# One block's k shift on 32x32 tiles of TensorE, with its result turned back by DMA

## The chip, the cores and the metric

The kernel runs on one core of a Trainium2 chip. The metric is the device time of one execution, in microseconds (us); lower is better. A core has five engines, each with its own in-order instruction queue: TensorE (PE, matmuls from SBUF into PSUM), VectorE (DVE), ScalarE (ACT), GpSimd (POOL) and SyncE (SP, which in this kernel only issues DMAs). An instruction that waits holds everything behind it on its engine.

## The reference, cut to what matters

Two layer pairs are applied to `x = A_q` of 2048 rows and 512 columns. The first of a pair is a gated long convolution, the second a SwiGLU FFN. All arrays are bf16.

```python
x = x + A(layernorm(x), k, v, shift_k, ssm_k, ssm_D)
x = x + B(layernorm(x), w_gate, w_up, w_down)
x = x + A(layernorm(x), ...)        # the same k, v and weights again
x = x + B(layernorm(x), ...)

def A(q, k, v, shift_k, ssm_k, ssm_D):
    # per channel: a causal filter of 4 taps over the rows of k
    k_shift[s] = sum(k[s - j] * shift_k[:, j] for j in range(4))
    kv = k_shift * v
    y = causal_conv(kv, ssm_k)      # by FFT, 2048 taps per channel
    return q * (y + kv * ssm_D)

def B(x, w_gate, w_up, w_down):     # 512 -> 1792 -> 512
    return (silu(x @ w_gate) * (x @ w_up)) @ w_down
```

The convolution doesn't depend on x, so the kernel computes it once and uses it in both layers.

## The kernel before, in words

**Tiles.** The 2048 rows are cut into 4 blocks of 512 (`NB = 4`). Inside a block, row 4p + r lies on partition p in slot r (`R = 4`), so a tile of a block is 128 x 4 x 512. 512 channels are 4 groups `dt` of 128.

**The convolution** (`conv(c)`, for blocks c = 1, 2, 3; block 0 is written out ahead of it). For each block: `spectrum_h` turns and transforms the long filter `hn` into `H`, `spectrum_x` shifts k, multiplies it into v (`vt`, in place) and transforms the product into `X`: for each slot r two matmuls of 512 columns (`by_residue`, L638) and an evacuation from PSUM to SBUF (L525). Products of spectra (`product`) run on VectorE, and `inverse` turns the sum back into `Yk`.

**The k shift** comes in two forms. Blocks 0 and 1 use `shift_mul` (L603 and on): k lies transposed in `kTb` (channels on partitions, 512 rows of time on the free axis, 16 more in front). For each slot r, 16 matmuls of 128 columns multiply a strided slice of `kTb` (the weights) with a diagonal matrix `dg` of one tap; the result has rows on the partitions, as `vt` has. For block 1, ScalarE copies it to `ks` (L620), and VectorE multiplies it into one slot of `vt` (L621). Four slots: four groups, four copies, four multiplies. Blocks 2 and 3 use `shift_mul_t` (L705 and on): ScalarE scales, VectorE adds, and DMAs turn the sum, 128 x 512 each, SBUF to SBUF.

**Units.** A unit (layer, block, half) is 256 rows through `prologue` (x += n * y, statistics, the normalised `z`, its transpose `zT`) and `ffn` (14 tiles of `w_gate` and `w_up`, then `w_down`). The first unit's prologue turns z on TensorE (L1022 to L1027); all others turn it by DMA (L994). The first unit needs the whole of block 0's convolution: products on VectorE, `inverse_half` (L881 and on, the matmuls L895 into two banks of ring `pd` and two of `pf`), `Yk` (L815), then x (L1004 to L1009), statistics (L914, L915), a power on GpSimd (L905), z (L964).

**PSUM** is cut into rings: `pf` 4 banks, `pc` 2, `pd` 2. In block 1, `shift_mul` takes `pc` banks one after the other.

**The order of the work** isn't found while the program runs. Each call of `plan.add` makes an operation with an engine, a modelled cost and, for DMAs, a modelled landing time `lat`. The list `ORDER` has one number for each operation, in the order of the `add` calls: its place. `Plan.order` sorts by place; `Plan.walk` models the run to choose buffers, and has rules of its own for when a transfer lands. Each engine then gets its operations in the order of their places, SP among them. The numbers were found by a search outside of the file. So a place decides what stands ahead of what on an engine.

**SP's queue.** All large loads and all turns by DMA, but for three small ones, are issued by SP in one queue: the first loads (L448, L458, L488, L492), `w_gate` (L503), the two turned tables `inv` (L1382, SBUF to SBUF), `kTb` of block 1 (L460, turned while it is loaded), `w_up` (L503), two parts of `w_down` (L500; 512 KB and 1280 KB), x of block 1 (L492), and, for block 2, `hn`, `kTb` and `vt`.

Of the kernel before, what the change touches and what calls it, by code (L numbers as in the profile page):

```python
# [9 lines left out]
P = 128  # L10
# [20 lines left out]
STRASSEN={(1,2,1):4,(0,3,0):4,(0,3,1):4,(1,3,0):4,(1,3,1):2}  # L31
I_RING = lambda k: "pf" if k == 3 else "pc"
# [88 lines left out]
R = 4  # L121
# [222 lines left out]
def kernel(  # L344
# [14 lines left out]
    nc = tc.nc  # L359
# [1169 lines left out]
```

## Time and profile before

| what | before |
|---|---|
| median of 3 runs | 339.6 us (339.44 to 339.8) |
| span of the profiled execution, first to last instruction | 337.7 us |
| what the median has above that span | 1.9 us |
| TensorE busy | 330.9 us, 98% |
| VectorE busy | 299.9 us, 89% |
| ScalarE busy | 262.8 us, 78% |
| granted TensorE clock | 1.000 |

The profiled execution has no time of its own beside its span, so the median of the runs is set beside the span. In the lines of the profile, `L416` is the line of kernel.py that issued an instruction (here the helper `mm`), PEld is TensorE's load of weights, `x16` a count, and `ps<-dg,kTb` says what was written from what. A timeline line begins with the start and the duration in us; in square brackets stands the idle time of the engine in front, and what ended it. `SPq` is SP issuing a DMA; its duration is the time that the issue took, while the landing time counts from issue to data landed. A line of the view of waits gives the sum, the count and the longest. A line of the view of windows gives the length of the stretch, then for each engine its busy time and count, the granted clock, the busy share of the DMA engines and GB/s.

### The profile page before, as it was taken

To read this page: it belongs to the slowest core of one execution; us is meant where nothing else is said; L and a number is where in the kernel's file an instruction comes from. 1 tells how busy PE (TensorE), PEld (TensorE's weight loads), DVE (VectorE), ACT (ScalarE), POOL (GpSimd) and SP (SyncE) were. 2 spreads that over 40 slices of the span, in tenths; PEclk is the share of its full clock that TensorE was granted. 3 is DMA by queue.
4 is the path that set the end of the run, shared out by engine and by line. 5 is a ranking of instruction groups with operands and counts; after the bars stand their busy time and mean duration, and the time that the engine had idled before them with its cause. 6 is when DMAs were issued, how large, how long until landed. Compare 5 with 4: busy or idle time off the path is not lost.

```text
span 337.7 us, 5898 instructions
## 1 busy us (share of the span) xinstructions
PE 330.9 (98%) x2141; PEld 204.6 (61%) x2172; DVE 299.9 (89%) x512; ACT 262.8 (78%) x534; POOL 35.4 (10%) x48
## 2 busy tenths in 40 slices
PE   9999999999999999999999999999999999999996
PEld 7655864645445564745454464744455687858884
DVE  8899999999888998999999999999999787877545
ACT  7889999999967466999899894999675556475462
POOL 4050001102100000122010100011100100100000
PEclk9999999999999999999999999999999999999999
DMA  7999604632346147421324434510514230204101
GB/s 255 350 229 376 130 13 66 151 82 41 71 93 94 36 91 188 95 49 32 62 53 106 97 60 110 138 35 16 96 28 82 56 72 17 48 18 93 49 3 62
DMA packets 77993, 31.59 MB, mean 94 GB/s; under 512 B 69766, under 2 KB 75787, under 8 KB 77963
## 3 DMA queue, kind: packets, MB, share of 16 engines
q1 hardware_dynamic: 77808, 31.13, 39.6%
q8 instruction: 17, 0.28, 0.4%
q14 instruction: 14, 0.11, 0.1%
q10 hardware_dynamic: 154, 0.07, 0.1%
HBM read 12.33 MB, written 2.10 MB: 43 GB/s over the span
## 4 chain that ended last, share of the span: by engine, by line
PE 91%; ACT 4%; DMA 2%; issue 1%; DVE 1%; SPq 1%
PE pf L416 56%; PE pd L1210 20%; PE ps L1085 7%; PE ps L416 6%; DMA kTb<-in_A_k_dram 1%; PE wm L1495 1%; DMA sg<-hr 1%; ACT H L525 1%; SPq L1132 1%; ACT ks L620 1%; ACT n L959 0%; ACT jk L929 0%; DVE t L748 0%; ACT ev L525 0%; ACT hr L1124 0%
## 5 line engine op out<-in xcount | busy, mean ns | idle before, releaser
L416 PEld LDWEIGHTS <-zT 128*128 128x128 bf16 x528 | 51.6, 98 | 58.5 <-DMA zT<-z 0.2
L416 PE MATMUL pf<-wg_sb,zT 128*128 128x512 bf16 x255 | 64.3, 379 | 0.5
L416 PE MATMUL pf<-wu_sb,zT 128*128 128x512 bf16 x260 | 64.3, 379 | 0.2
L1210 PE MATMUL pd<-wd_sb,sg 128*128 128x512 bf16 x189 | 48.1, 379 | 0.9 <-DMA sg<-hr 0.3
L1124 ACT CAST hr<-pf 128x512 bf16<-128x512 f32 x66 | 38.4, 593 | 12.4 <-PE pf L416 8.5
L1123 ACT ACTIVATE sg<-pf 128x512 bf16<-128x512 f32 x66 | 38.8, 608 | 11.3 <-PE pf L416 10.2
L416 PE MATMUL pf<-zT,wg_sb 128*128 128x256 bf16 x368 | 46.0, 273 | 0.1
L416 PE MATMUL pf<-zT,wu_sb 128*128 128x256 bf16 x368 | 45.9, 273 | 0.0
L758 DVE TENSOR_TENSOR t<-X,G 128x4096 bf16<-128x4096 bf16 x18 | 40.9, 2284 | 0.1
L416 PEld LDWEIGHTS <-wu_sb 128*128 128x128 bf16 x368 | 36.0, 98 | 8.1
L416 PEld LDWEIGHTS <-wg_sb 128*128 128x128 bf16 x368 | 35.9, 98 | 7.9 <-issue 0.4
L1183 ACT ACTIVATE sg<-pf 128x512 bf16<-128x512 f32 x46 | 27.3, 607 | 10.8 <-PE pf L416 10.8
L1187 ACT CAST ht<-pf 128x512 bf16<-128x512 f32 x46 | 26.8, 595 | 9.8 <-PE pf L416 8.0
L905 POOL TENSOR_TENSOR rstd<-mv,nhalf 128x2 f32<-128x2 f32 x20 | 17.0, 852 | 158.2 <-DVE mv L915 134.7
L1210 PEld LDWEIGHTS <-sg 128*128 128x128 bf16 x200 | 19.5, 98 | 21.7 <-DMA sg<-hr 0.8
L1210 PE MATMUL pd<-wd_sb,ht 128*128 128x512 bf16 (+1 forms) x124 | 29.7, 369 | 0.1
L914 DVE BATCH_NORM_STATS2 bst<-xc 128x6 f32<-128x512 bf16 x40 | 26.5, 683 | 0.5
L905 POOL TENSOR_TENSOR rstd<-ve,nhalf 128x2 f32<-128x2 f32 x12 | 14.6, 1218 | 111.7 <-ACT ve L942 111.7
L1190 DVE TENSOR_TENSOR ht<-ht,sg 128x512 bf16<-128x512 bf16 (+1 forms) x31 | 16.6, 544 | 8.8 <-ACT sg L1183 4.5
L1130 DVE TENSOR_TENSOR hr<-hr,sg 128x1024 bf16<-128x1024 bf16 x27 | 18.4, 682 | 4.2 <-ACT sg L1123 2.0
L1210 PEld LDWEIGHTS <-ht 128*128 128x128 bf16 x126 | 12.3, 98 | 13.1 <-DVE ht L1190 0.3
L525 ACT ACTIVATE X<-ps 128x512 bf16<-128x512 f32 x32 | 18.4, 604 | 1.6 <-PE ps L416 0.9
(143 smaller groups left out, 522.1 us busy)
## 6 DMA issues: line engine op xcount, KB each, us to landing
hn<-in_A_ssm_k_dram SPq DMA_DIRECT2D x4, 512.0 KB, 3.7
vt<-in_A_v_dram SPq DMA_DIRECT2D x4, 512.0 KB, 5.5
xc<-in_A_q_dram SPq DMA_DIRECT2D x4, 512.0 KB, 5.6
out_dram<-xc SPq DMA_DIRECT2D x15, 128.0 KB, 1.9
wg_sb<-in_B_w_gate_dram SPq DMA_DIRECT2D x1, 1792.0 KB
wu_sb<-in_B_w_up_dram SPq DMA_DIRECT2D x1, 1792.0 KB, 8.9
wd_sb<-in_B_w_down_dram SPq DMA_DIRECT2D x1, 1280.0 KB, 12.1
sg<-hr SPq DMA_TRANSPOSE x66, 2.4
```

The source lines that it names most:

```text
L416: nc.tensor.matmul(o, lhsT=lhsT, rhs=rhs, start=(n == 0), stop=(n == len(terms) - 1))
L525: add("ACT", act(D), lambda: nc.scalar.activation(out=view(), in_=ps.t[:], func=ACT.Copy, scale=scale), r=[ps], w=[(buf, keys)], conv=conv)
L758: dve(8 * D, lambda t=t, part=part: nc.vector.tensor_mul(out=t.t[:], in0=x.t[:, :, part:part + 1, :].to_broadcast((P, R, 2, D)), in1=g.t[: ...
L905: add("POOL", cost, lambda: nc.gpsimd.tensor_tensor(out=rstd.t[:], in0=var(), in1=nhalf.t[:].to_broadcast((P, n)), op=ALU.pow), r=reads + ...
L914: add("DVE", 0.6, lambda st=st, i=i: nc.vector.bn_stats(out=st.t[:, 0:6], in_=xs[c].t[:, i, :]), r=[(xs[c], (i,))], w=[st])
L1085: nc.tensor.matmul(bank.t[:, half_ * C:(half_ + 1) * C], lhsT=lhsT(i), rhs=rhs(i), start=(first and i == 0 and half_ == 0), stop=(last and ...
L1123: add("ACT", act(D), lambda ps=ps, dst=dst, o=o, which=which: nc.scalar.activation(out=rows(dst, o), in_=ps.t[:], func=ACT.Silu) if which ...
L1124: out=rows(dst, o), in_=ps.t[:], func=ACT.Silu) if which == "g" else nc.scalar.copy(out=rows(dst, o), in_=ps.t[:]),
L1130: dve(n * W, lambda: nc.vector.tensor_mul(out=hr.t[:], in0=hr.t[:], in1=sg.t[:]), [sg], [hr], due=(unit, k / pairs, 0.0, "h"))
L1183: add("ACT", act(D), lambda ps=ps, o=o, sg=sg: nc.scalar.activation(out=sg.t[:, o:o + 2, :], in_=ps.t[:], func=ACT.Silu), r=[ps], w=[(sg, ...
L1187: add("ACT", act(D), lambda ps=ps, o=o, ht=ht: nc.scalar.copy(out=ht.t[:, o:o + 2, :], in_=ps.t[:]), r=[ps], w=[(ht, (o // 2,))], due=(uni ...
L1210: nc.tensor.matmul((pds[o] if not cs.start else pds[HP]).t[:, cs], lhsT=ht.tiles(q, o), rhs=wt["d"].t[:, ft, cs], start=(ft == std0 and no ...
```

## The change

**1. Block 1's k shift** goes from `shift_mul` to a new `shift_mul_packed`. Now `kTb` is the moving operand and the 32 x 32 diagonal pieces of `dg` are the weights. For each tap, 16 matmuls of 512 columns, each on 32 rows and 32 columns of the array: row group i (32 channels of each dt) goes to PSUM bank i, channel group dt to 32 partitions of it. The result has channels on partitions, so ScalarE copies each bank into `kk` with the slots r apart, four DMAs turn 128 x 512 each, SBUF to SBUF, and two multiplies of 1024 go into `vt`, each on two of the four 32-channel pieces of all slots. The four banks are both of `pc` and both of `pd`, all at once.

```diff
+PACK, PACK_RINGS = 1.5, ("pc", "pc", "pd", "pd")
...
+    def shift_mul_packed(b, rings, after=()):
+
+        Q = P // R
+        pss = [new(ring, "ps", [P, L], F32) for ring in rings]
+        kk = new("s8", "kk", [P, 2, R, R, P], parts=2 * R)
+
+        def go():
+            for j in range(KS):
+                for i in range(R):
+                    rows = slice(i * Q, (i + 1) * Q)
+                    for dt in range(KD):
+                        nc.tensor.matmul(pss[i].t[dt * Q:(dt + 1) * Q, :], lhsT=dg.t[rows, dt, j, rows],
+                                         rhs=kT[b].t[rows, dt, PADL - j:PADL - j + L], start=(j == 0), stop=(j == KS - 1),
+                                         tile_position=(i * Q, dt * Q))
+        add("PE", PACK, go, r=[kT[b], dg], w=pss, conv=True, count=2 * KS * R * KD)
+        for i, ps in enumerate(pss):
+            add("ACT", 0.565, lambda i=i, ps=ps: nc.scalar.copy(out=kk.t[:, 0, i], in_=ps.t[:].rearrange("d (p r) -> d r p", r=R)),
+                r=[ps], w=[(kk, (i,))], conv=True)
+            add("SP", 1.29, lambda i=i: nc.sync.dma_start_transpose(out=kk.t[:, 1, i], in_=kk.t[:, 0, i]),
+                r=[(kk, (i,))], w=[(kk, (R + i,))], lat=1.17, conv=True)
+        for i in (0, 2):
+            v = lambda i=i: bass.AP(vt[b].t[:].tensor, vt[b].t[:].offset + i * Q, [vt[b].t[:].ap[0], [Q, 2], [P, R * KD], [1, Q]])
+            k = lambda i=i: kk.t[:, 1, i:i + 2].rearrange("p i r (k a) -> p i (r k) a", a=Q)
+            dve(2 * D, lambda v=v, k=k: nc.vector.tensor_mul(out=v(), in0=k(), in1=v()),
+                [(kk, (R + i, R + i + 1))], [vt[b]], conv=True, after=after)
+
     def spectrum_x(b):
         if K_ACT(b):
             shift_mul_t(b)
+        elif b == 1 and PACK:
+            shift_mul_packed(b, PACK_RINGS, stats)
         else:
             shift_mul(b, "pc", True, stats if b == 1 else ())
```

**2. Landing times** in the planner's model: `kTb` of block 1 from 3.7 to 4.9 us, x of block 1 from 10.5 to 14.5, `w_up` from 7.5 to 10.5, the two parts of `w_down` from 8.0 and 11.5 to 12.5 and 15.5. These numbers are the model's; the program that runs has them only through its order and its choice of buffers.

**3. `ORDER`** is another list throughout (1715 operations for 1716), and a small part of the statistics' buffer (`stat_slot`) is now made at its first use.

Numbering the `add` calls from 0, operations up to 252 are the same in both; 253 is the packed product; 254, 256, 258, 260 are the copies of banks 0 to 3 and 255, 257, 259, 261 their turns; 262 and 263 are the multiplies (banks 0 and 1, banks 2 and 3); what was 265 and up is now one less. The places around the change, as the two lists have them:

| operation | number now | place before | place now |
|---|---|---|---|
| SP: load of `kTb`, block 1 | 78 | 159 | 83 |
| SP: load of `w_up` | 79 | 161 | 84 |
| SP: load of `w_down`, second part | 81 | 187 | 85 |
| SP: load of x, block 1 | 286 | 190 | 87 |
| SP: load of `w_down`, first part | 80 | 237 | 90 |
| PE: k shift, block 1 | 253 | 166, 175, 212, 223 | 168 |
| ACT: copies of banks 3, 2, 1, 0 | 260, 258, 256, 254 | | 169, 170, 172, 177 |
| SP: turns of banks 3, 0, 1, 2 | 261, 255, 257, 259 | | 173, 178, 185, 226 |
| PE: first inverse matmul, block 0 | 186 | 176 | 180 |
| DVE: last statistics of the first unit | 215 | 213 | 221 |
| DVE: multiply, banks 0 and 1 | 262 | | 223 |
| DVE: z of the first unit | 220, 217 | 222, 218 | 224, 225 |
| DVE: multiply, banks 2 and 3 | 263 | | 227 |
| PE: turns of z | 221, 218 | 230, 228 | 231, 234 |
| DVE, ACT: copies into zT | 222, 219 | | 233, 237 |
| PE: first transforms of block 1's v | 268, 264 | | 235, 236 |
| PE: first FFN matmuls | 332 | 248 | 238 |
| SP: loads of v, `hn`, `kTb`, block 2 | 289, 287, 288 | | 247, 288, 309 |

Before, three transforms of block 1's v stood ahead of the first FFN matmul, and the load of `hn` of block 2 came right behind that of `w_down`'s first part on SP.

More of the change, by code (lines that the diff above doesn't have):

```diff
@@ L164, in buf, with add @@
         return b
-    def add(self, eng, cost, emit, r=(), w=(), lat=None, due=None, conv=False, slack=0.0, after=(), dest=None):
+    def add(self, eng, cost, emit, r=(), w=(), lat=None, due=None, conv=False, slack=0.0, after=(), dest=None, count=None):
         o = Op()
@@ L200, in add @@
                     break
+        o.count = count or o.count
         for b in o.bufs:
@@ L460, in load_k @@
         return add("SP", (2.6, 9.0, 4.4)[b - 1], lambda: nc.sync.dma_start_transpose(out=kT[b].t[:], in_=k3[b * L - PADL:(b + 1) * L]),
-            w=[kT[b]], lat=3.7 if b == 1 else 2.6, due=due, after=after)
+            w=[kT[b]], lat=4.9 if b == 1 else 2.6, due=due, after=after)
     def transpose_k(b, ring, engs):
@@ L491, in load_x @@
         xs[c] = new("x", "xc", [P, R, D], parts=R + 2)
-        return add("SP", 0.7, lambda: nc.sync.dma_start(out=xs[c].t[:], in_=q_t[:, c]), w=[xs[c]], lat=(7.5, 10.5, 5.0, 4.0)[c], due=due, after=after)
+        return add("SP", 0.7, lambda: nc.sync.dma_start(out=xs[c].t[:], in_=q_t[:, c]), w=[xs[c]], lat=(7.5, 14.5, 5.0, 4.0)[c], due=due, after=after)
     def load_weights(which, due, after=()):
@@ L500, in load_weights @@
                 o = add("SP", 0.6, lambda sl=sl: nc.sync.dma_start(out=wt[which].t[:, sl], in_=src[:, sl]), w=[(wt[which], (part,))],
-                        lat=(8.0, 11.5)[part], due=due, after=after)
+                        lat=(12.5, 15.5)[part], due=due, after=after)
             return o
-        return add("SP", 0.6, lambda: nc.sync.dma_start(out=wt[which].t[:], in_=src), w=[wt[which]], lat=7.5 if which == 'u' else 14.0, due=due, after=after)
+        return add("SP", 0.6, lambda: nc.sync.dma_start(out=wt[which].t[:], in_=src), w=[wt[which]], lat=10.5 if which == 'u' else 14.0, due=due, after=after)
     X, G, H, Y, Z = {}, {}, {}, {}, {}
@@ L907, in power, with stat_slot @@
         return rstd
+    def stat_slot(slot):
+        if bst.t is None:
+            bst.t = bst.make(0)
+        return bst.t[:, slot]
     def ln_stats(c, rows, pw=PW):
@@ L912, in ln_stats @@
         for o, i in enumerate(rows):
-            st = plan.buf("bn", "bnst", lambda slot: bst.t[:, slot])
+            st = plan.buf("bn", "bnst", stat_slot)
             add("DVE", 0.6, lambda st=st, i=i: nc.vector.bn_stats(out=st.t[:, 0:6], in_=xs[c].t[:, i, :]), r=[(xs[c], (i,))], w=[st])
```

131 rows, old and new, of the table ORDER are left out of this document.

## The prediction

> **What bounds the kernel now.** I read the page's totals first, then TensorE's share of the chain of work that ended last, then its waits from the point where the first FFN unit runs.
>
> ```profile
> span 337.7 us, 5898 instructions
> PE 330.9 (98%) x2141; PEld 204.6 (61%) x2172; DVE 299.9 (89%) x512; ACT 262.8 (78%) x534; POOL 35.4 (10%) x48
> PE 91%; ACT 4%; DMA 2%; issue 1%; DVE 1%; SPq 1%
> ```
>
> TensorE is busy 98% of the span and holds 91% of the chain. A busy TensorE may still have holes, since matmuls overlap; so here are its busy time from 32.88 us to 333 us (the sum over three stretches) and its only wait in that time, from the view of waits cut to it:
>
> ```profile
> sum 300.12, PE 298.37 PEld 182.10 DVE 269.82 ACT 234.36 POOL 26.40; mean PE 99.46 PEld 60.70 DVE 89.94 ACT 78.12 POOL 8.80
> PE pd L1210 <- DMA sg<-hr: 0.3, 1, 0.3
> ```
>
> One wait of 0.3 us in 300 us: behind 32.88 us TensorE is full, and in order. So the kernel is two parts: the time at which the first FFN matmul starts, and a full TensorE queue behind it. A change moves the end in just two ways: it moves that start, or it changes the TensorE work queued behind it. A new search of the orders has 0.3 us to win there, no more.
>
> What sets the start is read in the timeline around it (start, duration, engine, line; x is a count):
>
> ```profile
> 22.76 1.08 PE L416 MATMUL ps<-dg,kTb 128*128 128x128 bf16 x16 [0.82 <-DMA kTb<-in_A_k_dram]
> 24.63 1.89 DVE L889 TENSOR_TENSOR m<-Z 128x1024 bf16<-128x1024 bf16 x3
> 25.00 0.38 PE L895 MATMUL ps<-m,inv 128*128 128x512 bf16 x1
> 30.10 0.73 DVE L621 TENSOR_TENSOR vt<-ks,vt 128x512 bf16<-128x512 bf16 x2
> 31.08 0.73 DVE L964 TENSOR_SCALAR z<-xc,mv,rstd 128x512 bf16<-128x512 bf16 x2 [0.25 <-POOL rstd L905]
> 31.55 0.72 PE L1022 MATMUL ptz<-ident,z 128*128 128x128 bf16 x8
> 32.31 0.42 DVE L1025 COPY zT<-ptz 128x512 bf16<-128x512 bf16 x1 [0.16 <-PE ptz L1022]
> 32.88 1.03 PE L416 MATMUL pf<-zT,wg_sb 128*128 128x256 bf16 x8
> ```
>
> The first k shift group (L416, the helper `mm`) starts when `kTb` lands; the inverse transform of block 0 starts at 25.00, when VectorE has `m`; VectorE then updates x, takes statistics, multiplies two rows of block 1's v (L621), writes z (L964); z is turned, copied, and the FFN starts at 32.88, which is 7.9 us behind the inverse's start. L621 stands ahead of z on VectorE and costs 0.73 us, because `ks` is there in time.
>
> **The change, part by part.**
>
> *TensorE.* Removed: 4 groups of 16 products of 128 columns. Added: 64 products of 512 columns on 32x32 tiles. Rows of the chain of waits for their pace, and one line's weight loads:
>
> ```profile
> 0.78 2.72 PE wm L1495 x24
> 3.49 0.22 PE pt L1358 x4
> 5.78 0.89 PE pt L472 x16
> 22.76 1.10 PE ps L416 x16
> 125.07 5.18 PE pd L1210 x24
> L1210 PEld LDWEIGHTS <-ht 128*128 128x128 bf16 x126 | 12.3, 98 | 13.1 <-DVE ht L1190 0.3
> ```
>
> A removed group takes 0.89 to 1.10 us: 3.6 to 4.4 us for four. No row shows 32x32 tiles. Lower end: 16 at once, 64/16 passes of 5.18/24 = 0.216 us: 0.9 us. Upper end: none at once, 64 x 0.216 = 13.8 us, and 20.1 us if each waits for its own weights too (64 x 0.098). The nearest row for the bare pair of instructions is the tap turn (four pairs on 4 rows and 4 columns, 0.22 us, 0.055 each), at a time when 128 columns take 2.72/24 = 0.113 us; later they take 0.89/16 = 0.056, half. Half of 0.055 for 64 pairs is 1.8 us, which I take. It starts at 22.76 as before, in place of the first group, and ends near 24.6, ahead of the inverse. So it saves about 2 us of TensorE time, but all of it ahead of the FFN's start, where TensorE is not what is late.
>
> *ScalarE and the PSUM banks.* Four copies out of PSUM before, four after. But the packed product fills both `pd` banks, and the inverse of block 0 needs these two: it now waits for copies 260 and 258, which the table puts on ScalarE behind an evacuation, the normalised row 110 and one more evacuation. Their rows:
>
> ```profile
> 23.88 0.59 ACT L620 CAST ks<-ps 128x512 bf16<-128x512 f32 x1 [0.78 <-PE ps L416]
> 24.36 1.09 ACT L525 ACTIVATE H<-ps 128x512 bf16<-128x512 f32 x2
> 25.32 1.52 ACT L959 ACTIVATE n<-xc,nmr,rstd 128x512 bf16<-128x512 bf16 x2
> ```
>
> Row 110 can start when VectorE has its shift, near 24.7: 0.76, an evacuation 0.55 and two copies 0.59 end near 27.2. The inverse then starts 2.2 us later than at 25.00, and the last statistics near 32.4 instead of 30.2. Below, this is hidden by a longer wait; without that cover it costs up to 2.2.
>
> *The turns, on SP.* Counting the calls of `add`, 253 is the packed product, 254/255 to 260/261 are copy and turn of the four PSUM banks, 262 and 263 the two multiplies by v. By the table's places SP now runs: both `inv`, `kTb` of block 1, `wu`, the second part of `wd` (81), x of block 1 (286), the first part of `wd` (80, place 90), then the four turns 261, 255, 257, 259 (places 173, 178, 185, 226), and only then `vt`, `hn` and `kTb` of block 2. What such a queue does is in SP's timeline and in the issue-to-landing times (last number, us):
>
> ```profile
> 4.54 13.09 SPq L1382 DMA_TRANSPOSE inv<-fwd  x2
> 17.68 2.68 SPq L460 DMA_TRANSPOSE kTb<-in_A_k_dram  x1
> 20.41 0.58 SPq L503 DMA_DIRECT2D wu_sb<-in_B_w_up_dram  x1
> 21.59 4.26 SPq L492 DMA_DIRECT2D xc<-in_A_q_dram  x1
> 25.89 0.43 SPq L500 DMA_DIRECT2D wd_sb<-in_B_w_down_dram  x1
> 26.43 2.68 SPq L448 DMA_DIRECT2D hn<-in_A_ssm_k_dram  x1
> 29.30 7.83 SPq L460 DMA_TRANSPOSE kTb<-in_A_k_dram  x1
> ...
> inv<-fwd SPq DMA_TRANSPOSE x2, 14.7
> zT<-z SPq DMA_TRANSPOSE x30, 2.4
> wd_sb<-in_B_w_down_dram SPq DMA_DIRECT2D x1, 512.0 KB, 9.9
> kTb<-in_A_k_dram SPq DMA_TRANSPOSE x1, 11.3
> 27.50:30.00 2.50, 2.50 (x26) 1.61 (x24) 2.36 (x7) 2.50 (x6) 0.00 (x0) 1.00 1.08 366
> ```
>
> A turn in an empty queue lands in 2.4 us (`zT`). The same kind of transfer, SBUF to SBUF, issued at 4.54 behind the loads of the prologue took 14.7 us (`inv`), and the transposed load issued at 29.30 behind `wd` and `hn` took 11.3. So transfers of this queue go in order, and a turn lands behind the loads ahead of it. The last of these is `wd`'s first part: issued at 25.89, landed 9.9 later, at 35.8. The queue moves 366 GB/s there, so nothing but its bytes is late, and the change leaves these bytes as they are.
>
> The four turns move 4 x 128 KB. Early end: right behind `wd` at 366 GB/s, 0.36 us each: the third at 36.9, the fourth at 37.2. Late end: `kTb` of block 2, as many bytes, landed at 29.30 + 11.3 = 40.6 with `hn` ahead of it (0.52 MB, 1.4 us), which now comes later: the fourth at 39.2, and, with a quarter of the 3.4 us behind 35.8 for each, the third at 38.3. I take the middles: 37.6 and 38.2.
>
> *VectorE, the wait that is added.* The table puts 262 at place 223, between the last statistics (215 at 221) and z (220 and 217 at 224 and 225), and 263 behind z at 227. 262 needs the turns 255 and 257, the second and third. VectorE works in order: behind 262 wait z, for z TensorE's turn of z, for that the FFN. On TensorE two products with block 1's v (268, 264) also stand ahead of the first FFN matmul (332), and need 263. The row for a multiply or an add of 1024, the length of 262 and 263:
>
> ```profile
> 44.25 0.68 DVE L987 TENSOR_TENSOR xc<-xc,n 128x1024 bf16<-128x1024 bf16 x1
> ```
>
> From the third turn at 37.6: multiply 0.68 from 37.7 to 38.4; z 0.73 to 39.1; the second multiply 0.68 to 39.8 (its turn landed at 38.2); the copy of zT 0.42 to 40.2; the FFN 0.15 later (32.88 less 32.73 in the trace), at 40.4 with rounding. Before it was 32.88: **7.5 us later.** If the multiplies' 32-wide pieces are slower than a plain 1024, each adds a few tenths.
>
> *Behind the start.* The first FFN matmul had three products of block 1's v ahead of it and now has two: one more behind, 0.2 us. The stall swallows the 2 us saved on TensorE.
>
> *Landing times and orders.* The new landing numbers are what the planner believes; they move nothing on the chip except by the order. The order behind the FFN's start can win 0.3 us and lose more; I take nothing.
>
> **Sum:** 337.7 + 7.5 + 0.2 = 345.4 us of span; the median of the runs, 339.6, is 1.9 above this span: **347.3 us.**
>
> **Rivals.**
>
> *The turns come in time (faster).* If a turn does not queue behind the loads, the last one lands 2.4 us behind a copy near 28, so near 30.5, when VectorE is at its statistics. Then the FFN's start is set as before by inverse, statistics and z. If ScalarE also frees the banks by 25, the inverse, no longer broken up by k shift groups, may bring the FFN forward by 1.0 us, less 0.2: 338.8 us. It is between 339.8 (nothing won, 0.2 lost) and 337.0 (all of 4.4 - 1.8). For it: 2.4 us in an empty queue. Against: 14.7 and 11.3 behind loads. It decides if the third turn lands before about 30.5.
>
> *The turns come in time, but the banks don't (a little slower).* The inverse 2.2 later, 1.0 won back, 0.2: 341.0 us, at most 342.0.
>
> *The tiles do not run at once (slower still).* No row tells. At 13.8 us the packed product ends at 36.6, the inverse starts there at the earliest, and the FFN 7.9 later at 44.5: 11.6 later, and 351.4 in all; with weights in the open, 20.1 us, 357.7. It decides from some 7 to 9 us on; below that the turns are later anyway.
> [...]
>
> *The loads land sooner (slower by less).* From `kTb`'s landing at 22.7 the four loads ahead (4.19 MB) need 11.4 us at 366 GB/s: 34.1, not 35.8. Then all comes 1.7 earlier: 345.6; with turns at their early end 344.9. It needs an even spread over the DMA engines.
>
> **How the numbers follow.** Forecast, with the sooner loads: 0.77, own range 344 to 349. Turns in time: 0.14, of which 0.02 ends within 0.2% of 339.6. Banks alone: 0.04. Tiles one by one: 0.05. A measurement here tells 0.2% (0.7 us) from no change. Faster 0.12, same 0.02, slower 0.86. The range goes down to 341.0 for the banks alone and up to 351.5 for the near end of the serial tiles.
>
> **What would show it.** In the changed profile: VectorE idle for some 7 us ahead of the first vt multiply, ended by a DMA into `kk`; turns with 6 to 11 us from issue to landing against 2.4 for `zT`; the first FFN matmul near 40.4 instead of 32.88; TensorE idle about 8 us ahead of it; no new wait behind it. The packed product near 1.8 us would right the tile step. It is wrong if the turns land in about 2.5 us, if `wd`'s first part lands far before 35.8, or if VectorE isn't where the wait is.

## The result, and the profile after

The changed kernel takes **349.58 us** (median; 348.93 to 351.12) against 339.6 us of the kernel before, run beside it (339.44 to 339.8): a ratio of 1.0301, 95% interval 1.0277 to 1.0325. It is slower by 10 us. The forecast was 347.3, range 341.0 to 351.5.

The page of the profiled execution (348.93 us of device time), totals and shares of the chain that ended last:

```profile
span 347.1 us, 5890 instructions
PE 331.2 (95%) x2139; PEld 201.9 (58%) x2172; DVE 300.3 (86%) x510; ACT 263.4 (76%) x534; POOL 35.3 (10%) x48
PE 62%; DVE 19%; ACT 7%; DMA 6%; issue 3%; SPq 1%; POOL 1%; DVEq 0%; POOLq 0%
```

TensorE has as much to do as before (331 us) in a span 9.4 us longer, and its share of the chain fell from 91% to 62%: it waits now. Where, the timeline around the start of the FFN tells (start, duration, engine, line; in brackets the idle time in front and what ended it):

```profile
23.02 1.14 PE L742 MATMUL ps<-kTb,dg 32*32 32x512 bf16 x64
23.50 0.85 ACT L997 ACTIVATE n<-xc,nmr,rstd 128x512 bf16<-128x512 bf16 x1
24.68 2.10 ACT L747 CAST kk<-ps 128x512 bf16<-128x512 f32 x4
25.36 0.38 PE L928 MATMUL ps<-m,inv 128*128 128x512 bf16 x1 [0.88 <-ACT kk L747]
30.49 0.31 DVE L953 BATCH_NORM_AGGREGATE mv<-bst 128x2 f32<-128x9 f32 x2
35.46 0.69 DVE L754 TENSOR_TENSOR vt<-kk,vt 128x1024 bf16<-128x1024 bf16 x1 [4.66 <-DMA kk<-kk]
36.07 0.73 DVE L1002 TENSOR_SCALAR z<-xc,mv,rstd 128x512 bf16<-128x512 bf16 x2
36.54 1.03 PE L1060 MATMUL ptz<-ident,z 128*128 128x128 bf16 x8 [5.59 <-DVE z L1002]
38.26 1.55 PE L421 MATMUL pf<-zT,wg_sb 128*128 128x256 bf16 x8
```

The packed product is short (1.14 us) and the inverse of block 0 starts at 25.36, 0.36 us later than before. The last statistics (L953) are done at 30.8. Then VectorE stands at the multiply into `vt` and waits 4.66 us for a DMA into `kk`; z comes behind it, TensorE stands idle for 5.59 us, and the first FFN matmul runs at 38.26 instead of 32.88. Two durations have grown as well: the eight turns of z take 1.03 us instead of 0.72, the first eight FFN matmuls 1.55 instead of 1.03.

The reason for the late turns is in SP's timeline, then in the issue-to-landing time of the last load ahead of them (last number), then in the piece of the chain ahead of the multiply (start, duration):

```profile
15.88 2.30 SPq L465 DMA_TRANSPOSE kTb<-in_A_k_dram  x1
24.84 0.43 SPq L505 DMA_DIRECT2D wd_sb<-in_B_w_down_dram  x1
25.37 3.18 SPq L749 DMA_TRANSPOSE kk<-kk  x1
```

```profile
wd_sb<-in_B_w_down_dram SPq DMA_DIRECT2D x1, 512.0 KB, 8.9
```

```profile
30.16 5.22 DMA kk<-kk
```

`wd`'s first part, issued at 24.84, lands 8.9 us later, at 33.7. The four turns stand behind it; the third is issued at 30.16 and lands at 35.38.

The clock is what stretched the short matmuls. The view of windows, one line for each us (the number behind the brackets of POOL is the granted clock):

```profile
35.00:36.00 1.00, 0.00 (x0) 0.00 (x0) 0.54 (x1) 0.00 (x0) 0.00 (x0) 0.95 0.93 129
36.00:37.00 1.00, 0.46 (x5) 0.47 (x6) 1.00 (x4) 0.00 (x0) 0.00 (x0) 0.50 0.83 270
37.00:38.00 1.00, 1.00 (x8) 0.65 (x6) 1.00 (x3) 0.39 (x1) 0.00 (x0) 0.50 0.98 353
38.00:39.00 1.00, 1.00 (x6) 0.54 (x4) 1.00 (x2) 0.97 (x4) 0.00 (x0) 0.50 1.08 349
39.00:40.00 1.00, 1.00 (x10) 0.81 (x9) 1.00 (x1) 0.97 (x4) 0.00 (x0) 0.85 1.28 248
```

From 35.9 us, still in the idle stretch, to 39.3 us TensorE is granted half its clock (0.95 in the first of these lines leaves 0.1 us of half clock, 0.85 in the last one 0.3).

So 5.4 us of the 9.4 lie ahead of the first FFN matmul. The other 4.0 lie behind it. TensorE's waits from 38.5 to 333 us, and its busy time from 60 to 333 us (sum over three stretches), of the changed kernel and, in the third fence, of the kernel before:

```profile
PE pd L1248 <- DMA sg<-hr: 1.8, 2, 1.1
PE pf L421 <- ACT hr L1162: 0.3, 1, 0.3
```

```profile
sum 273.00, PE 269.28 PEld 159.13 DVE 243.04 ACT 206.22 POOL 28.16; mean PE 89.76 PEld 53.04 DVE 81.01 ACT 68.74 POOL 9.39
```

```profile
sum 273.00, PE 271.41 PEld 164.04 DVE 242.91 ACT 207.54 POOL 23.97; mean PE 90.47 PEld 54.68 DVE 80.97 ACT 69.18 POOL 7.99
```

About as many matmul records are missing in both (33 and 31 of 2172), so the two sums can be compared: 2.1 us more idle TensorE. The waits shown hold 2.1 us against 0.3 before, 1.8 of them for turned rows (`sg<-hr`). The transform that moved behind the start is 0.2, the half clock behind 38.26 about 0.5. Some 1.2 us of the 4.0 are left. Of these, 0.5 stand behind TensorE's last matmul: from its end to the end of the span it is 3.5 us (343.62 to 347.1), before 3.0 (334.66 to 337.7). The rest isn't placed line by line; the experiments place the whole by edits.

### The profile page after: what moved, and what is told of

Its sections match the earlier page's. It is cut to its first block, busy times and chain, and to the rows that moved or that the text cites. A ratio compares the mean times of both kernels' runs of the same rounds, so it can differ in the third digit from the quotient of the medians.

```text
span 347.1 us, 5890 instructions
## 1 busy us (share of the span) xinstructions
PE 331.2 (95%) x2139; PEld 201.9 (58%) x2172; DVE 300.3 (86%) x510; ACT 263.4 (76%) x534; POOL 35.3 (10%) x48
## 4 chain that ended last, share of the span: by engine, by line
PE 62%; DVE 19%; ACT 7%; DMA 6%; issue 3%; SPq 1%; POOL 1%; DVEq 0%; POOLq 0%
PE pf L421 35%; PE pd L1248 13%; PE ps L1123 7%; PE ps L421 4%; DVE t L791 4%; DMA sg<-hr 4%; DVE m L651 2%; PE ps L569 2%; DMA kk<-kk 2%; DVE hr L1168 1%; DMA kn<-in_A_k_dram 1%; DVE t L795 1%; DVE Z L799 1%; DVE ka L719 1%; ACT jk L976 1%
## 5 line engine op out<-in xcount | busy, mean ns | idle before, releaser
L421 PE MATMUL pf<-wu_sb,zT 128*128 128x512 bf16 x255 | 63.4, 379 | 0.8 <-ACT hr L1162 0.3
L1248 PE MATMUL pd<-wd_sb,sg 128*128 128x512 bf16 x187 | 47.4, 379 | 2.6 <-DMA sg<-hr 1.8
L1162 ACT CAST hr<-pf 128x512 bf16<-128x512 f32 x66 | 37.5, 596 | 13.6 <-PE pf L421 9.3
L421 PE MATMUL pf<-zT,wg_sb 128*128 128x256 bf16 x368 | 46.9, 274 | 0.1
L1135 ACT CAST mt<-ps 128x512 bf16<-128x512 f32 (+1 forms) x20 | 10.1, 535 | 14.1 <-PE ps L1123 14.0
```

Of the source, the lines that this page charges most:

```text
L421: nc.tensor.matmul(o, lhsT=lhsT, rhs=rhs, start=(n == 0), stop=(n == len(terms) - 1))
L1162: out=rows(dst, o), in_=ps.t[:], func=ACT.Silu) if which == "g" else nc.scalar.copy(out=rows(dst, o), in_=ps.t[:]),
L1248: nc.tensor.matmul((pds[o] if not cs.start else pds[HP]).t[:, cs], lhsT=ht.tiles(q, o), rhs=wt["d"].t[:, ft, cs], start=(ft == std0 and no ...
```

## The experiments

**Theory A**: there are two causes; the turns, late behind the loads, cost what the start is later, and the new list costs the other 4 us behind the start, whatever the k shift. **Theory B**, the rival: there is one cause, the late start, and what is lost behind it follows from it. Times are medians; the kernel before ran beside each group, at 339.46 to 339.73 us.

### What the wait costs: four ways to take it away

**The multiplies read the copies as they are, not turned; the turns are issued and nobody waits for them.**

```diff
-            k = lambda i=i: kk.t[:, 1, i:i + 2].rearrange(...)
+            k = lambda i=i: kk.t[:, 0, i:i + 2].rearrange(...)
-                [(kk, (R + i, R + i + 1))], [vt[b]], conv=True, after=after)
+                [(kk, (i, i + 1))], [vt[b]], conv=True, after=after)
```

> The changed kernel, but the two multiplies read the ScalarE copies before they are turned, so nobody waits for the turns; the four turns are still issued. (Block 1's k shift therefore enters v unturned.) Theory A: the stall ahead of the first FFN matmul is all that the late turns cost, 5.4 us and some tenths of slow clock, and the other 4 us lie in the new orders: first FFN matmul near 33, time 343 to 344.5. Theory B: the 4 us behind the start follow from the stall (engines out of step, clock): first FFN matmul near 33, time 339 to 340.3.

Measured: 344.68 us (344.37 to 346.01), ratio 1.0156 (1.0133 to 1.0179). The first FFN matmul runs at 33.73. TensorE's waits from 34 to 333 us:

```profile
PE pd L1248 <- DMA sg<-hr: 2.4, 2, 1.4
PE pf L421 <- ACT hr L1162: 0.3, 1, 0.3
```

The wait is gone and 4.9 us with it; the time is 0.2 above A's range. The waits behind the start are the same two as in the changed kernel, so they don't come from the stall, and the time is 4.4 us above B's range: B falls here.

**The loads of the second part of `w_down`, of x and of the first part of `w_down` move behind the four turns on SP.** (`moved` puts operations behind another one in the order.)

```diff
+ORDER = moved(ORDER, ([81, 286, 80], 259))
```

> The changed kernel, with the loads of the second part of w_down, of x of block 1 and of the first part of w_down moved behind the four turns on SP's queue; w_up stays ahead of them. Whole computation. Theory A (the turns land late because of the loads that stand ahead of them in one queue): turns land 2.5 to 4 us after their issue, the third one by 31.5, the first FFN matmul at 33.5 to 35.0, time 344.0 to 346.0; what stays above before, some 5 us, belongs to the new orders. Rival (a turn of this kind is slow by itself, four at a time): landing 4.6 to 6 us as now, first FFN at 37.5 to 38.5, time 348.5 to 350. The loads come 5 to 8 us later; if x of block 1 or w_down is then late, a wait for it shows behind the start, with up to 2 us.

Measured: 344.58 us (343.36 to 345.37), ratio 1.0139 (1.011 to 1.0169). The timeline of SP and of the FFN's start, the turns' landing times in the view of the tile `kk`, then TensorE's first wait and its busy time behind the start:

```profile
24.91 5.83 SPq L763 DMA_TRANSPOSE kk<-kk  x4
30.79 0.58 SPq L519 DMA_DIRECT2D wd_sb<-in_B_w_down_dram  x1
33.40 1.91 PE L435 MATMUL pf<-zT,wg_sb 128*128 128x256 bf16 x8
```

```profile
DMA to landing us min/median/max: 2.4/2.5/3.3
```

```profile
PE pd L1262 <- DMA sg<-hr: 2.0, 2, 1.2
```

```profile
sum 273.00, PE 270.55 PEld 160.42 DVE 239.98 ACT 204.88 POOL 27.82; mean PE 90.18 PEld 53.47 DVE 79.99 ACT 68.29 POOL 9.27
```

With no `w_down` and no x ahead of it, the same turn lands in 2.5 us. The loads ahead of the turns are the cause, and their price, 349.58 less 344.58, is **5.0 us** by the medians, the same as with the wait taken out. Whether a turn waits for its place in the queue or for busy DMA engines, this edit doesn't tell, since it takes away both. The loads are issued 7 to 12 us later now, and no wait for them shows on TensorE behind the start.

**The two multiplies stand behind block 1's last step for `H` on VectorE, and block 1's transforms behind them.** (In the trace they run at 36.56, z at 30.51.)

```diff
+ORDER = moved(ORDER, ([262, 263], 247), ([268, 264, 269, 265, 278, 272, 279, 273], 263))
```

> The changed kernel with the whole computation; in the order the two multiplies go behind block 1's last H step on VectorE, and the first four transforms of block 1's v behind them on TensorE. The turns land as late as before, but z does not stand behind them. Theory A: first FFN matmul near 33, no stall ahead of it, time 343 to 344.5. Theory B: 339 to 340.5. If the turns' own lateness counts wherever they stand, the wait moves to the transforms and the time stays over 347.

Measured: 346.96 us (344.5 to 348.15), ratio 1.0206 (1.0163 to 1.0249), 2.5 above A's range. The FFN starts at 32.50, earlier than in any other run, and yet the kernel is slower than with the loads moved. TensorE's waits from 32.5 us on:

```profile
PE pd L1262 <- DMA sg<-hr: 2.0, 2, 1.1
PE pf L435 <- ACT zT L1079: 0.8, 1, 0.8
PE ps L435 <- ACT X L544: 0.7, 1, 0.7
PE pf L435 <- ACT sg L1235: 0.4, 1, 0.4
```

The wait for `zT` is the one right ahead of the start; those for `X` and `sg`, 1.1 us, stand behind it, where the run with the loads moved has 0.2 for `sg`. So what the edit takes from the start it gives back, with block 1's transforms moved. The profiled execution is the fastest of the four (344.5) and alone has a clock of 0.999; the three others (346.9 to 348.15) have 0.995. What they have above it beside the clock, no trace shows.

**ScalarE issues the turns on its own queue.**

```diff
-            add("SP", 1.29, lambda i=i: nc.sync.dma_start_transpose(out=kk.t[:, 1, i], ...
+            add("ACT", 1.29, lambda i=i: nc.scalar.dma_start_transpose(out=kk.t[:, 1, i], ...
```

> The changed kernel, with the four turns issued by ScalarE on its own queue instead of by SP, at the same places of the order; the loads stay as they are. Whole computation. It tells two readings of the late turns apart. If a turn waits because its queue carries the loads in order, it lands 2.4 to 3.5 us after its issue on another queue, the first FFN matmul comes at 33.5 to 35.0, and the time is 344 to 346, as with the loads behind the turns. If it waits because the 16 DMA engines are full of loads whatever the queue, it lands after 4.5 us or more, the third one near 35, and the time stays at 348 to 351. In both cases ScalarE spends 1.2 us or more on each issue, which delays its next evacuations.

Measured: 360.7 us (359.25 to 361.84), ratio 1.0622 (1.0593 to 1.0651). Both readings missed. The chain from 26 us on (start, duration):

```profile
26.59 12.05 DMA kTb<-in_A_k_dram
...
38.79 1.28 ACTq L749
```

ScalarE stood still for 14.3 us: its first turn was issued 0.15 us after `kTb` of block 2, a turned load on SP's queue, had landed, and then landed in 2.5 us. The chain has that landing right in front of the turn; why ScalarE stood until then, no view of this run shows. Whether a turn on another queue would pass the loads themselves stays open: it never got to try.

### What the new list costs

**The new list and landing times, with the old k shift** (four groups, copies and multiplies in the places of the packed product, its copies and its multiplies).

```diff
-PACK, PACK_RINGS = 1.5, ("pc", "pc", "pd", "pd")
+PACK, PACK_RINGS = 0, ("pc", "pc", "pd", "pd")
+ORDER = unpacked(ORDER)
```

> The changed kernel's landing times and orders with the old k shift (four groups of 128-column products, no turns) put at the same places. Theory A (the 4 us are the new orders'): first FFN matmul near 33, time 343 to 344.5, within 0.5 of the run in which nobody waits for the turns, because the 2 us of TensorE time that packing saves lie ahead of the FFN's start. Theory B: 339 to 340.3. If saved TensorE time counts anywhere: 2 us above the run in which nobody waits.

Measured: 345.49 us (344.95 to 346.38), ratio 1.0175 (1.0152 to 1.0197). Without a turn in it, the new list is still 5.9 us slower than the old one; that is 1.0 above A's range, and 0.8 above the run in which nobody waits. Part of that is the old k shift in places that weren't chosen for it (the FFN starts at 35.60); the wait for `sg<-hr` behind the start is there too, 1.3 us.

**The loads behind the turns as above, and from the first FFN matmul on the old list.** (One transform of block 1's v goes back to its old, later place. The kernel has the finished list; the lines say in short how it comes about. One more transform and its evacuation come a few places later than in the old list.)

```diff
+head, tail = seq[:at], seq[at:] + [268]      # at: behind the first FFN matmul
+tail.sort(key=lambda o: OLD[o])              # place in the list of before
```

> The run with the loads behind the turns, and beside that, from the first FFN matmul on, the operations in the order of the list of before; up to there the new list stands, but for one transform of block 1's v that goes back to its old, later place. Whole computation. Theory A (the new list costs 4 to 5 us behind the start): first FFN matmul at 33.0 to 34.0, less than 1.5 us of idle TensorE behind it, time 340.0 to 342.0 against 344.6 with the new list behind the start. Rival (the new list's holes come from what the head leaves behind: a later v of block 1, later loads): holes as before, time 343.5 to 345.5.

Measured: 342.53 us (341.08 to 343.11), ratio 1.0075 (1.0051 to 1.0099): 0.5 above the expected range. Against the run with the new list behind the start, the edit brings **2.05 us** by the medians. But the two runs don't have the same clock: that one had 0.995 in two executions (345.3 on average) and 0.999 to 1.000 in two (343.6), this one 0.994 in three (342.7) and 1.000 in one (341.1). At like clock, that is among executions with the same granted clock, the edit brings 2.5 to 2.6 us. TensorE's waits behind 33.5 us, and its busy time from 60 to 333:

```profile
PE pf L418 <- ACT sg L1218: 0.5, 1, 0.5
PE ps L418 <- ACT X L527: 0.3, 1, 0.3
```

```profile
sum 273.00, PE 273.00 PEld 163.60 DVE 242.77 ACT 209.81 POOL 24.67; mean PE 91.00 PEld 54.53 DVE 80.92 ACT 69.94 POOL 8.22
```

273.00 of 273.00 us, where the new list had 270.55 (both traces have all 2172 matmuls): every hole behind 60 us was the list's, 2.45 us in all, as much as the edit brings at like clock. Theory A had 4 to 5 us for it; the size was much too large, and its sum left out the half clock, which holds 1.2 us of the rest (below).

**The whole old list, with the packed shift put into it**: the product in the place of the first old group, the turns behind the first part of `w_down`, the multiplies behind a small step of the next unit (they run at 41.72), block 1's first transforms behind them. The planner's landing times are not those of before, as the expectation has it, but still the changed kernel's. The kernel has the finished list; the line says in short how it comes about.

```diff
+put(253, place_of_old=259); put([261, 259, 257, 255], behind=80); put([262, 263], behind=230)
```

> The packed k shift with the order list and landing times of before: the product stands where the old first group stood, the four turns stand behind the first part of w_down on SP, the two multiplies stand behind the first copy into zT on VectorE, and block 1's transforms behind them. Whole computation. Theory A (the new orders cost about 5 us, the stall the rest; the packed shift itself saves nothing that counts): first FFN matmul at 32.9 to 34.0, time 339.8 to 341.8. Rival 1 (the packed shift itself costs, by its four banks or the turns, whatever the order): over 344. Rival 2 (its 2 us less of TensorE come out at the end once nothing waits for it): below 339.0.

Measured: 342.69 us (341.99 to 344.07), ratio 1.008 (1.0061 to 1.0099), 0.9 above the expected range. The timeline at the start, and the first wait behind it:

```profile
32.06 0.72 PE L1057 MATMUL ptz<-ident,z 128*128 128x128 bf16 x8 [2.01 <-DVE z L999]
33.39 1.86 PE L418 MATMUL pf<-zT,wg_sb 128*128 128x256 bf16 x8 [0.39 <-DVE zT L1060]
```

```profile
PE pf L418 <- ACT sg L1218: 1.3, 1, 1.3
```

The shorter product doesn't bring the FFN forward: TensorE waits 2.01 us for z instead, and the first FFN matmuls then take 1.86 us instead of 1.03, at half clock (0.50 granted from 34 to 36 us). The time that was saved came back as idle time, and half clock followed it.

### What TensorE's time ahead of the start is worth

**Before, with one tap instead of four in block 1** (12 of each 16 products left out).

```diff
-                        for j in range(KS)])
+                        for j in range(1 if b else KS)])
```

> The kernel before, but block 1's k shift computes one tap of four: 48 of its 64 products of 128 columns are left out, 2.7 us of TensorE time at 0.056 each. If what is saved ahead of the first FFN matmul isn't on the path: first FFN matmul within 0.4 of 32.88 and a time of 339.0 to 339.8. If TensorE time counts wherever it is: 336.9.

Measured: 341.93 us (341.51 to 342.19), ratio 1.007 (1.0053 to 1.0087), above the range for either case. Less work made it slower: the FFN starts 0.26 earlier (32.62), but new holes appear behind the start, among them 0.9 us of waits for `sg<-hr`. The edit also takes out 96 instructions, so it doesn't measure TensorE's time alone.

**The same with all instructions kept: three taps' products cover 16 of 128 columns.**

```diff
+                            n = 16 if j else P
+                            nc.tensor.matmul(ps.t[:, dt * P:dt * P + n], lhsT=..., rhs=dg.t[:, dt, j, 0:n], ...)
```

> The kernel before, with as many instructions as it has: in block 1's k shift the products of taps 1 to 3 cover 16 of the 128 columns, so that TensorE has about 2 us less to do ahead of the first FFN matmul (it leaves out three taps for 112 columns of each 128; the result isn't the reference's). Theory A (TensorE's time ahead of the start isn't on the path there): first FFN matmul within 0.4 us of 32.88, time 339.0 to 339.8. Rival (TensorE's time counts wherever it is saved): first FFN about 1.5 to 2 us earlier, time 337.4 to 338.2. On the run with one tap, which had 2.4 us of new idle TensorE behind the start: if the missing 96 instructions shifted the fine order there, no such holes appear here; if it was the shorter k shift itself, they appear again, and the time is 341 to 342.

Measured: 339.56 us (339.11 to 340.04, 10 runs), ratio 1.0002 (0.9992 to 1.0012). The timeline:

```profile
22.61 0.77 PE L612 MATMUL ps<-dg,kTb 128*128 128x128 bf16 x16
31.93 0.38 PE L416 MATMUL ps<-vt,fwd 128*128 128x512 bf16 x1 [0.74 <-ACT ks L626]
33.59 1.03 PE L416 MATMUL pf<-zT,wg_sb 128*128 128x256 bf16 x8
```

A group takes 0.77 us instead of 1.08, four groups 1.2 us less, and nothing follows: TensorE waits for ScalarE instead (and 1.1 us for VectorE's `m`), and the first FFN matmul is not earlier (33.59, against 33.28 at the latest expected). So 1.2 us saved on TensorE ahead of the start are worth nothing. The packed product saves more there, 3.1 us (four groups of 1.06 to 1.08 for 1.14); that all of it is worth nothing is not shown by this run, but in no run with the packed product does the FFN start more than 0.4 us earlier than before. No holes appear behind the start, which points to the fewer instructions of the run with one tap, and not to its shorter work. That isn't shown, since one tap saved 2.7 us and this run 1.2; by what way the holes come stays open.

### What the clock costs

**Changed kernel, 25 matmuls that nobody reads ahead of the first turn of z.**

```diff
+            if o.n == 221:
+                fill_up(...)      # 25 x [128 x 512], weights of ones
```

> The changed kernel, with 25 more matmuls of 512 columns that nobody reads, put on TensorE ahead of the first turn of z, where it waits for 5.6 us. Whole computation. If the idle stretch costs a stretch of half clock behind it (0.50 from 36 to 39 us, which takes about 1.5 us of work at the start), the clock stays near 1.0 from 36 to 39, the first FFN matmul runs at 37.6 to 37.9 and the time is 347.9 to 348.9. If the half clock comes whatever TensorE does, or costs nothing because the start waits for VectorE, the time is 349.3 to 350.2. Should the 25 matmuls outlast the wait, the start is later by what is left of them, at most 0.5 us.

Measured: 350.03 us (349.41 to 351.24), ratio 1.0307 (1.0283 to 1.0331): no gain, though the clock stayed at 0.998 to 1.000 (0.985 to 0.994 without them). The timeline:

```profile
30.27 5.55 PE L1540 MATMUL wm<-wg_sb,const-bfloat16-1.0 128*128 128x512 bf16 x25
37.13 0.72 PE L1062 MATMUL ptz<-ident,z 128*128 128x128 bf16 x8 [1.30 <-DVE z L1004]
38.53 1.03 PE L423 MATMUL pf<-zT,wg_sb 128*128 128x256 bf16 x8
```

The turns of z take 0.72 again. But z came 0.59 later in this execution (37.13 for 36.54), because VectorE waited 6.0 us for the turn instead of 4.7, and 2.9 us of waits for `sg<-hr` follow, 1.8 in the changed kernel. The time lies in the range of the reading by which the clock costs nothing; but with two other waits in charge, the clock's price can't be read from this run.

**The same in the old list with the packed shift**, 8 matmuls ahead of operation 221.

> The packed shift in the order list of before, with 8 more matmuls of 512 columns that nobody reads, ahead of the first turn of z, where TensorE had nothing to do from 30.05 to 32.06 us. Whole computation. If that idle stretch, which the shorter product leaves, is what halves the clock behind it, the granted clock stays at 1.0 from 33 to 37, and the time goes from 342.7 to 341.0 to 341.6 (1.5 us of work at the start less; the wait of 1.46 us for ScalarE at 45 us stays, and is before's order not fitting). If the clock is granted back without a gain in time, as in the run with 25 more matmuls, it stays at 342.3 to 343.0.

Measured: 344.64 us (344.06 to 345.68), ratio 1.0155 (1.0135 to 1.0175). The time lies above both expected ranges, and the run says nothing of the clock's price. In the old list 221 is the second turn of z, so the eight stood between the two turns and pushed the FFN back from 33.39 to 34.48:

```profile
31.39 0.40 PE L1059 MATMUL ptz<-ident,z 128*128 128x128 bf16 x4 [2.00 <-DVE z L1001]
31.63 1.89 PE L1537 MATMUL wm<-wg_sb,const-bfloat16-1.0 128*128 128x512 bf16 x8
33.57 0.38 PE L1059 MATMUL ptz<-ident,z 128*128 128x128 bf16 x4
```

**Once more where no other wait is left**: loads behind the turns, old list behind the start, and 6 matmuls ahead of 221, which is the first turn there.

> The run with the loads behind the turns and the old order behind the start, with 6 more matmuls of 512 columns that nobody reads, ahead of the first turn of z, where TensorE had nothing to do from 30.77 to 32.19 us; three of that run's four executions had a granted clock of 0.994 (342.31 to 343.11 us), one of 1.000 (341.08). Whole computation. If the idle stretch halves the clock and the half clock sets the start, the clock is 1.0 in all executions and the time 340.8 to 341.4; with the three waits of 1.3 us that remain behind the start it is still above before. If the clock costs nothing, because what it holds up waits for another engine anyway, the time stays at 342.2 to 342.9.

Measured: 341.37 us (340.97 to 341.53, 5 runs), ratio 1.0049 (1.0035 to 1.0063), against 342.53 without the six. All five executions have a clock of 0.999 or 1.000. The same microsecond in the view of windows, without the six (first fence) and with them (second):

```profile
34.00:35.00 1.00, 1.00 (x6) 0.69 (x5) 1.00 (x2) 0.64 (x3) 0.00 (x0) 0.50 1.22 325
```

```profile
34.00:35.00 1.00, 1.00 (x10) 0.68 (x8) 1.00 (x1) 0.77 (x2) 0.00 (x0) 1.00 0.93 272
```

Work that nobody reads makes the kernel **1.2 us** faster, by the clock: the one execution without the six that kept a clock of 1.000 took 341.08 us, as little as those with them. It is the best packed version found, and still 0.5% behind the kernel before.

### The sum

| step back | us | what it takes away |
|---|---|---|
| changed kernel | 349.58 | |
| loads behind the turns | 344.58 | 5.0: the turns wait for the loads |
| old list behind the start | 342.53 | 2.05: new waits for turned rows |
| clock kept | 341.37 | 1.2: half clock behind the idle stretch |
| kernel before, beside it | 339.73 | 1.6: all that is left of the change |

The steps are differences of medians, and the second row mixes two clocks. Among executions with a clock of 0.994 to 0.995 that row has 345.3 and the third 342.7: then the first step is 4.3 us, the second 2.6 and the third 1.35. (The changed kernel's own clock is lower still in three of its four executions, 0.985 to 0.990.)

The last 1.6 are not the packed shift's alone: up to the FFN's start the new list still stands, and the landing times are the new ones. Of them, the start of the FFN is 0.35 (33.23 for 32.88), and the profile shows waits of 0.8 for ScalarE's `sg`, 0.5 for its `zT` (ahead of the first FFN matmul, so part of the 0.35) and 0.3 for its `X`.

## Why the prediction was right in sign and off in its parts

**The frame** (a start, and a full TensorE queue behind it) was right for the kernel before and for what moved the start. It was taken too far: that the queue *was* full is no promise that another list keeps it full.

**The packed product**: 1.8 taken, 1.14 measured, near the low bound (0.9). Rightly off the path: the run with narrow taps shows that 1.2 us saved there give nothing. The rival of tiles that don't run at once is out: 64 products took 1.14 us and not 13.8, and their 64 weight loads, 0.84 us in all, lie inside of that time and not in the open.

```profile
23.02 0.84 PEld L742 LDWEIGHTS <-dg 32*32 32x32 bf16 x64 [0.74 <-issue]
```

**The PSUM banks**: the mechanism is there (TensorE waits 0.88 us for ScalarE's copy), the size was 0.36 us of later inverse instead of 2.2. ScalarE ran row, evacuation and copies in the order of the list, but the row started at 23.50 and not near 24.7, and the inverse's first matmul went on behind the first copy (24.68 to 25.36), not the second.

**The turns behind the loads**: right, and the term that carries the sign. The last load landed at 33.7 and not at 35.8, since the whole queue ran about 2 us earlier than before (`kTb` issued at 15.88 for 17.68, landed 4.8 us later for 5.0); the prediction had kept the old times for it. From that landing to the third turn 1.8 us were forecast and 1.6 measured. The turns show 3.0 to 6.1 us from issue to landing, not 6 to 11, because SP itself was held: the first issue took 3.18 us, and the later turns were issued later.

**VectorE's order**: right. From the third turn to the first FFN matmul 2.8 us were forecast, 2.88 measured, with 0.3 of half clock in it. So the start is 5.4 us later and not 7.5. The rival with loads that land sooner had this size (345.6), by another way.

**"The order behind the FFN's start can win 0.3 us and lose more; I take nothing"**: this is the step that failed. It lost 2.05 us by the one edit (2.5 to 2.6 at like clock), and the half clock, which the prediction didn't have at all, takes 1.2. The forecast ended 2.3 below the time: 2.1 too much at the start stood against 3.8 too little behind it (0.2 forecast, 4.0 measured), and the median lies 2.5 above the profiled span, where 1.9 were taken. That the time came this near, and into the range, is luck in part. With the start as it was measured, the same sum gives 345.2, which is 4.4 too low.

**"No new wait behind it"** was the mark that the profile of the changed kernel should show, and it doesn't: TensorE waits 1.8 us for `sg<-hr` behind the start, where the kernel before has 0.3.

## What to carry to other kernels

A DMA on the path must be placed by what stands ahead of it in its queue, not by its own time: the same turn landed in 2.5 us with the loads behind it and in 4.6 with them ahead of it (medians of four), and the kernel took some 5 us longer. Time saved on an engine that will wait anyway was worth nothing (1.2 us less for TensorE ahead of the start, 339.56 us for 339.6), and on TensorE it could cost, since half clock came with idle stretches of 1.42, 2.01 and 5.59 us, though not with one of 1.52 (1.2 us of time where it could be told). Where an order was found by search for a full engine, a new list is a cost of its own: put the old list back behind the change and see what is left.

## What the runs showed of the hardware

The prediction had no term for the clock, and a pause of 1.42 us, with shorter ones beside it, could be followed by half of it. One line each of the timeline with the loads behind the turns and the old list, and of the run with one tap:

```profile
32.19 0.72 PE L1057 MATMUL ptz<-ident,z 128*128 128x128 bf16 x8 [1.42 <-DVE z L999]
```

```profile
30.96 0.38 PE L416 MATMUL ps<-vt,fwd 128*128 128x512 bf16 x1 [1.52 <-ACT ks L620]
```

The first was followed by a half clock (0.50 granted from 34 to 36 us; the mean over the span was 0.994 in three of four executions, 1.000 in the fourth), the second wasn't (1.00 in each us from 30 to 38, 0.999 to 1.000 over the span in all four executions), so the length of one pause doesn't settle it. And 64 matmuls of 512 columns on 32x32 tiles, 16 places of the array, took 1.14 us, where four of 512 columns on the whole array take 1.03 in the same trace (L569 at 20.01 us).
